# Attention and MLP on one core: heads in pairs on the full array, zero-padded keys, attention merged with the preceding batch's MLP

## The chip, the cores and the metric

The kernel runs on one core of a Trainium2 chip. The metric is device time in microseconds (us), the median of several executions. The engines have short names in the profile: PE (TensorE, matrix products), PEld (its weight loads), DVE (VectorE), ACT (ScalarE), POOL (GpSimd) and SP (SyncE, which here only issues loads and stores). "Span" is the time from a profiled execution's first instruction to its last; the time of an execution is about 2 us more. The numbers of the profile are of one profiled execution of each kernel.

## The reference, cut to what matters

```python
# q, k, v: (8 batches, 12 heads, 448 positions, 64), float32
q_n, k_n = rmsnorm(q, g_q), rmsnorm(k, g_k)          # over the 64, with 1e-6
scores = q_n @ k_n.T / 8;  attn = softmax(scores)
x = (attn @ v) laid out as (3584 tokens, 768)
h = x @ w_in                                         # 768 -> 2048
g = h * clip(h + 3, 0, 6) / 6
out = g @ w_out                                      # 2048 -> 768, float32
```

## The kernel before

It takes a batch at a time. First it loads all twelve heads and finds all their norms, then it runs through the heads one by one, and between the heads it places pieces of the MLP of the batch before. Positions are cut into four tiles of 112. Both weights are loaded first, ahead of q and k, and cast on POOL.

```python
for kt in range(NKT):                                    # both weights, before any q or k
    nc.sync.dma_start(out=st[:], in_=moe_w_in[...])
    nc.gpsimd.tensor_copy(out=w_in_sb[:, kt, :], in_=st[:])
...
for h in range(H):                                       # loads and squares of all heads
    ...
    nc.gpsimd.tensor_tensor(out=sq[:], in0=qk_sb[:], in1=qk_sb[:], op=A_MULT)       # L190
    nc.vector.tensor_reduce(out=ssq_all[:, h, :], in_=sq[:], axis=X, op=A_ADD)      # L191
nc.scalar.activation(out=rstd_all, in_=ssq_all, func=LN, ...)    # then EXP, scale -0.5
...
# per head: transposes of q and k (L225, L227), then for each of 4 key tiles
nc.tensor.matmul(out=sc_ps[:], lhsT=kT[:, j * PP:(j + 1) * PP], rhs=qpT[:], ...)    # L241: 64 rows
nc.scalar.activation(out=eT[:], in_=sc_ps[:], func=EXP, scale=rstd_all[...])        # L246
# 16 products of probabilities and values (L258), then the division (L265, L266)
...
# MLP pieces of batch b-1 between the heads: h (L103), activation (L110, L111), y (L125)
```

## Time and profile before

| | before |
|---|---|
| time, median of 4 runs beside the changed kernel | 773.21 us (768.98 to 775.74) |
| PE busy, 0 to 75 us | 0.8 us |
| PE busy, 200 to 300 us | 99.0 us |
| one batch in the middle | about 77 us |

The first lines are the page's first part (busy time of each engine over the span) and its slices, each of 1/40 of the span, with the busy share in tenths:

```profile
span 768.0 us, 12093 instructions
...
PE 643.1 (84%) x4672; PEld 388.0 (51%) x4672; DVE 356.5 (46%) x946; ACT 358.3 (47%) x608; POOL 136.3 (18%) x222
...
PE   0000999698999999998999899989999999987566
...
POOL 5544311232411211121112111210000000000000
```

PE does nothing for four slices and is then nearly always busy. The windows view gives the same by stage, with the number of instructions behind each busy time, then the granted TensorE clock (1.00 is full speed; this trace has no clock records before 160 us, where the view says 1.00), the DMA share and GB/s:

```profile
0.00:75.00 75.00, 0.80 (x9) 0.80 (x10) 22.58 (x42) 3.22 (x4) 38.26 (x54) 1.00 0.79 232
200.00:300.00 100.00, 99.00 (x782) 61.28 (x781) 61.64 (x164) 58.34 (x100) 21.69 (x35) 1.00 0.32 79
```

The waits view (who waited for whom: total us, times, longest) says what the start is: one single wait, for the scaled queries, that come only after all norms of a batch and after both weights.

```profile
PE qkT_ps L225 <- DVE qs_bf L209: 74.2, 1, 74.2
```

The groups by shape (line, engine, operation, output<-inputs, shapes, count, then busy us and mean ns of one, and idle time before with its releasers) give what the operations take:

```profile
L103 PE MATMUL h_ps<-xT_sb,w_in_sb 128*128 128x448 bf16 x768 | 177.0, 362 | 25.4 <-DVE gT L111 24.8 <-DVE xT_sb L299 0.5
L241 PE MATMUL sc_ps<-qpT,kT 64*112 64x448 bf16 x384 | 141.4, 416 | 10.5 <-DVE kT L233 7.5 <-ACT eT L246 3.1
...
L258 PEld LDWEIGHTS <-eT 112*112 112x112 bf16 x1536 | 101.9, 141 | 51.2 <-issue 21.2 <-PE sc_ps L241 20.3 <-PE qkT_ps L227 2.0
L190 POOL TENSOR_TENSOR sq<-qk_sb 112x512 f32<-112x512 f32 x96 | 101.5, 1062 | 146.2 <-DMA qk_sb<-in_k_dram 95.6 <-DVE qs_bf L209 20.4 <-DVE ssq_all L191 19.3
...
L103 PEld LDWEIGHTS <-w_in_sb 128*128 128x128 bf16 x768 | 69.9, 100 | 93.7 <-issue 45.5 <-POOL v_aug L217 1.0
```

A matmul's recorded time is longer than its share of a stream of matmuls (362 ns for L103 above, with starts 189 ns apart), so I also took the distance from each matmul's start to the start of the next in the trace. Medians from 200 to 600 us: 189 ns within L103 (448 columns), 52 ns within L258, 49 ns within a run of transposes. The score matmul L241 also streams 448 columns, but with 64 rows: its median is 279 ns.

### The profile page before, as it was taken

The numbers are of one execution on the slowest core, as the hardware profiler recorded it, in microseconds if no ns is written. First come the engines' busy times: TensorE is split into PE (matmuls) and PEld (weight loads), VectorE is DVE, ScalarE is ACT, GpSimd is POOL, SyncE is SP. The second block draws the span as 40 slices with busy tenths as digits, with TensorE's granted clock in tenths as the row PEclk, the third lists the DMA queues.
The fourth block names the chain that finished last, engine by engine and source line by source line (L and its number), as shares of the span: only waits on it lengthen the run. The fifth ranks groups of instructions, "written<-read, shape, count | busy, mean of one in ns | idle before, by whom it ended". The sixth has DMA issues, their size and how long they took to land.

```text
span 768.0 us, 12093 instructions
## 1 busy us (share of the span) xinstructions
PE 643.1 (84%) x4672; PEld 388.0 (51%) x4672; DVE 356.5 (46%) x946; ACT 358.3 (47%) x608; POOL 136.3 (18%) x222
## 2 busy tenths in 40 slices
PE   0000999698999999998999899989999999987566
PEld 0000565354566556655665566556755665554234
DVE  1226535767846763666357643754255324411210
ACT  0001446357655673566456644664466546621221
POOL 5544311232411211121112111210000000000000
PEclk9999999999999999999999989998999999999999
DMA  7787701714433323331333223320100010011001
GB/s 277 239 219 188 164 1 33 159 32 104 102 81 84 79 49 93 82 72 45 79 91 73 54 60 92 80 54 25 46 10 1 19 55 2 1 37 36 1 18 54
DMA packets 141113, 57.41 MB, mean 75 GB/s; under 512 B 134656, under 2 KB 134656, under 8 KB 140288
## 3 DMA queue, kind: packets, MB, share of 16 engines
q1 hardware_dynamic: 141056, 56.65, 28.6%
q8 instruction: 36, 0.59, 0.3%
q14 instruction: 21, 0.17, 0.1%
HBM read 45.61 MB, written 11.01 MB: 74 GB/s over the span
## 4 chain that ended last, share of the span: by engine, by line
PE 79%; DMA 6%; ACT 6%; DVE 5%; POOL 2%; issue 1%; SPq 0%; ACTq 0%; DVEq 0%; POOLq 0%
PE y_ps L125 22%; PE h_ps L103 20%; PE sc_ps L241 15%; PE av_ps L258 13%; PE qkT_ps L225 4%; PE qkT_ps L227 3%; DMA wst_out<-in_moe_w_out_dram 3%; DMA wst_in<-in_moe_w_in_dram 2%; DVE gT L111 2%; ACT t_sb L110 2%; PE xT_ps L294 2%; DVE qs_bf L209 1%; ACT L201 1%; ACT L197 1%; ACT y_sb L131 1%
## 5 line engine op out<-in xcount | busy, mean ns | idle before, releaser
L246 ACT ACTIVATE eT<-sc_ps,rstd_all 112x448 bf16<-112x448 f32 x384 | 230.7, 632 | 84.5 <-PE sc_ps L241 82.8
L125 PE MATMUL y_ps<-w_out_sb,gT 128*112 128x256 bf16 (+1 forms) x1024 | 197.3, 329 | 9.6 <-ACT y_sb L131 7.2
L103 PE MATMUL h_ps<-xT_sb,w_in_sb 128*128 128x448 bf16 x768 | 177.0, 362 | 25.4 <-DVE gT L111 24.8
L241 PE MATMUL sc_ps<-qpT,kT 64*112 64x448 bf16 x384 | 141.4, 416 | 10.5 <-DVE kT L233 7.5
L125 PEld LDWEIGHTS <-gT 128*112 128x112 bf16 x1024 | 120.4, 130 | 58.9 <-issue 16.1
L111 DVE SCALAR_TENSOR_TENSOR gT<-t_sb,h_ps 128x448 bf16<-128x448 f32 x128 | 78.9, 617 | 143.2 <-ACT t_sb L110 102.1
L110 ACT ACTIVATE t_sb<-h_ps,half_c 128x448 f32<-128x448 f32 x128 | 81.1, 634 | 122.1 <-PE h_ps L103 113.8
L258 PEld LDWEIGHTS <-eT 112*112 112x112 bf16 x1536 | 101.9, 141 | 51.2 <-issue 21.2
L190 POOL TENSOR_TENSOR sq<-qk_sb 112x512 f32<-112x512 f32 x96 | 101.5, 1062 | 146.2 <-DMA qk_sb<-in_k_dram 95.6
L258 PE MATMUL av_ps<-v_aug,eT 112*112 112x65 bf16 x1536 | 118.8, 228 | 0.3 <-ACT eT L246 0.3
L103 PEld LDWEIGHTS <-w_in_sb 128*128 128x128 bf16 x768 | 69.9, 100 | 93.7 <-issue 45.5
L225 PE MATMUL qkT_ps<-identity,qs_bf 112*64 112x112 bf16 x384 | 44.8, 234 | 74.2 <-DVE qs_bf L209 74.2
L131 ACT COPY y_sb<-y_ps 112x512 f32<-112x512 f32 x64 | 30.6, 479 | 128.7 <-PE y_ps L125 106.5
L191 DVE TENSOR_REDUCE ssq_all<-sq 112x8 f32<-112x512 f32 x96 | 64.2, 675 | 41.5 <-POOL sq L190 41.1
L225 PEld LDWEIGHTS <-qs_bf 112*64 112x64 bf16 x384 | 26.8, 118 | 92.5 <-DVE qs_bf L209 74.2
L241 PEld LDWEIGHTS <-kT 64*112 64x112 bf16 x384 | 41.9, 132 | 60.7 <-issue 39.2
L217 POOL MEMSET v_aug<- 112x4 bf16 x96 | 10.3, 117 | 283.9 <-PE av_ps L258 276.2
L209 DVE TENSOR_TENSOR qs_bf<-qk_sb,rstd_all 112x256 bf16<-112x256 f32 x96 | 42.4, 460 | 26.9 <-ACT rstd_all L201 17.0
L231 DVE TENSOR_SCALAR qpT<-qkT_ps,gprime 64x448 bf16<-64x448 bf16 x96 | 42.0, 438 | 27.4 <-PE qkT_ps L227 21.4
L265 DVE RECIPROCAL rden<-av_ps 112x4 f32<-112x4 f32 x96 | 17.3, 180 | 79.7 <-PE av_ps L258 79.7
L215 DVE CAST k_bf<-qk_sb 112x256 bf16<-112x256 f32 x96 | 36.2, 380 | 34.0 <-DMA qk_sb<-in_k_dram 34.0
L227 PE MATMUL qkT_ps<-identity,k_bf 112*64 112x112 bf16 x384 | 45.6, 232 | 0.0
(24 smaller groups left out, 240.9 us busy)
## 6 DMA issues: line engine op xcount, KB each, us to landing
qk_sb<-in_q_dram SPq DMA_DIRECT2D x96, 112.0 KB, 2.6
qk_sb<-in_k_dram SPq DMA_DIRECT2D x96, 112.0 KB, 2.7
v_sb<-in_v_dram SPq DMA_DIRECT2D x96, 112.0 KB, 2.2
out_dram<-y_sb SPq DMA_DIRECT2D x32, 336.0 KB, 2.7
wst_in<-in_moe_w_in_dram SPq DMA_DIRECT2D x6, 1024.0 KB, 5.1
wst_out<-in_moe_w_out_dram SPq DMA_DIRECT2D x16, 384.0 KB, 3.8
gq_t<-in_g_q_dram SPq DMA_DIRECT2D x1, 0.2 KB, 2.3
gk_t<-in_g_k_dram SPq DMA_DIRECT2D x1, 0.2 KB, 2.3
```

The costliest lines, as they stand in the source:

```text
L103: nc.tensor.matmul(out=h_ps[:], lhsT=w_in_sb[:, kt, f * 128:(f + 1) * 128], rhs=xT_sb[:, kt, bb * S:(bb + 1) * S], start=(kt == 0), stop=( ...
L110: nc.scalar.activation(out=t_sb[:], in_=h_ps[:], func=RELU, bias=half_c[:, :], scale=1.0 / 6.0)
L111: nc.vector.scalar_tensor_tensor(out=gT[:, f, :], in0=t_sb[:], scalar=1.0, in1=h_ps[:], op0=A_MIN, op1=A_MULT,)
L125: nc.tensor.matmul(out=y_ps[:], lhsT=gT[:, f, mt * PP:(mt + 1) * PP], rhs=w_out_sb[:, f, n0:n1], start=(f == 0), stop=(f == NFT - 1),)
L190: nc.gpsimd.tensor_tensor(out=sq[:], in0=qk_sb[:], in1=qk_sb[:], op=A_MULT)
L191: nc.vector.tensor_reduce(out=ssq_all[:, h, :], in_=sq[:], axis=mybir.AxisListType.X, op=A_ADD,)
L209: nc.vector.tensor_tensor(out=qs_bf[:], in0=qk_sb[:, 0:NJ, :], in1=rstd_all[:, h, 0:NJ].unsqueeze(2).to_broadcast([PP, NJ, D]), op=A_MULT,)
L225: nc.tensor.transpose(qkT_ps[:, j * PP:(j + 1) * PP], qs_bf[:, j, :], identity[:])
L227: nc.tensor.transpose(qkT_ps[:, (NJ + j) * PP:(NJ + j + 1) * PP], k_bf[:, j, :], identity[:])
L241: nc.tensor.matmul(out=sc_ps[:], lhsT=kT[:, j * PP:(j + 1) * PP], rhs=qpT[:], start=True, stop=True,)
L246: nc.scalar.activation(out=eT[:], in_=sc_ps[:], func=EXP, bias=0.0, scale=rstd_all[:, h, NJ + j:NJ + j + 1],)
L258: nc.tensor.matmul(out=av_ps[:, i, 0:D + 1], lhsT=expT[j][:, i * PP:(i + 1) * PP], rhs=v_aug[:, j, :], start=(j == 0), stop=(j == NJ - 1),)
```

## The change

Its intent is to fill the array. Two heads form a pair, so that q and k of a pair have 128 rows; the keys of one head of the pair are padded with zeros in the rows of the other, so that each score matmul runs over the full array. Positions are cut into three tiles of 128, and the last 64 positions ("odd rows") of both heads share one tile. The attention's output comes out by token and is normalised with one division per pair. MLP work goes in small pieces between the attention's pieces, in proportion to its cost. The weights are cast by the DMA, the norms are found on POOL with a power instead of on ACT, and the scaling of q and k moves from DVE to POOL. (Nearly the whole body is new; this is its core.)

```diff
-    nc.scalar.activation(out=rstd_all[:], in_=ssq_all[:], func=LN, ...)
-    nc.scalar.activation(out=rstd_all[:], in_=rstd_all[:], func=EXP, bias=0.0, scale=-0.5)
+    def rstd_of(ssq, n):
+        nc.gpsimd.tensor_scalar(ms[:], ssq, 1.0 / D, 1e-6, A_MULT, A_ADD)              # L128
+        nc.gpsimd.tensor_tensor(out=rs[:], in0=ms[:], in1=npow[:, 0:n], op=A_POW)      # L130
+    def load_pair(P): ...                                                              # L138, L141
+    def prep_pair(P):
+        nc.gpsimd.tensor_tensor(out=sq[:], in0=qk_flat, in1=qk_flat, op=A_MULT)        # L150
+        nc.vector.tensor_reduce(out=ssq[:], in_=sq..., axis=AX_X, op=A_ADD)            # L152
+        rs = rstd_of(ssq[:], 4 * NT)
+        for i in range(2):
+            nc.gpsimd.tensor_tensor(out=qks[:, i]..., in0=qk[:, i]..., in1=rs4...)     # L158
+        nc.gpsimd.tensor_copy(out=va[:, :, :, 0:D], in_=vf...)                         # L164
+    def trans_pair(P):                      # 6 transposes (L241), q copied (L243)
+        for a in range(2):                  # keys times 1 or 0 by half: the padding
+            nc.vector.tensor_scalar_mul(kp[:, a, :], ps[:, 1]..., gmask[:, a:a + 1])   # L247
+    def score(P, u):                        # 7 a pair
+        nc.tensor.matmul(out=ps[:], lhsT=lhsT, rhs=st["qT", b][:, j, :], ...)          # L263
+        nc.scalar.activation(out=st["e", P][:, u, :], in_=ps[:], func=EXP, ...)        # L264
+    # av: products with the values (L272, L275), division (L289, L291); xtrans (L329, L330)
-qk_pool bufs=H, bf_pool bufs=H
+qk_pool = pool("qk_pool", 4);  qks_pool = pool("qks_pool", 4);  sq_pool = pool("sq_pool", 2)
+    def att_items(P):
+        items = [(0.0, lambda: load_step(P + 4)), (0.0, lambda: prep_step(P + 3)),
+                 (0.36, lambda: trans_step(P + 2))]
+        ...                                 # score(P + 1, u) merged with av(P, t), xtrans(P)
+    for P in range(4): load_step(P)
+    for kt in range(NKT): nc.gpsimd.dma_start(out=w_in_sb[:, kt, :], in_=moe_w_in[...])  # casts
+    for P in range(3): prep_step(P)
+    for ft in range(0, NFT, 4): nc.gpsimd.dma_start(out=w_out_sb[...], in_=moe_w_out[...])
+    for b in range(B):
+        mlp = merge(h_items(b - 1), y_items(b - 2))
+        for _, fn in merge(att, mlp): fn()
```

## The prediction

> **What bounds the kernel now.** TensorE, after a late start. The chain of waits is 79% PE, and the windows show PE 98 to 99% busy from 200 to 600 us, DVE 47 to 62%, ACT 56 to 58%, POOL 5 to 22%. In the first 75 us PE is busy 0.8 us: weights are loaded ahead of q and k, and the first transpose waits 74.2 us (waits view) for the normalised queries of all twelve heads. Later a batch takes about 77 us. From matmul start to next matmul start the trace has, as medians, 189 ns for L103 (448 columns), 215 and 109 ns for L125 (512, 256), 52 ns for L258, 49 ns for a transpose, but 280 ns for the score matmul L241, which also streams 448 columns with 64 rows: about 90 ns more than a full-height one, x384 = 35 us.
>
> **What changes, in PE time, estimated from those distances.**
> - Scores: 384 x 280 ns = 107 us become 336 x 189 = 64 us: heads of a pair share one full-height tile, and the 64 odd keys of both heads make one matmul.
> - Attention x values: 1536 x 52 = 80 us become 1344 x about 50 = 67 us. The Trainium skill, "TensorE: Matmul & The Clock Gate", section "Weight-path perf modes", says fast weight load needs 128 weight columns. The trace agrees: 100 to 107 ns for 128 columns, 130 to 141 ns for 112.
> - Transposes: 960 x 49 = 47 us become 504 x 56 = 28 us.
> - h: same columns, 145 us. y: 28 row tiles instead of 32, 166 us become 896 x 162 = 145 us.
> Sum 545 before, 449 after: 56 us a batch. I add 8% for idle: about 61 us a batch against 77.
>
> **What moves.** DVE's scaling and casts go to POOL, weight casts into the DMA; the Ln/Exp table loads (19 us of ACT) go. The weights are loaded behind the first pairs, so attention starts near 25 us. But POOL then has per pair: square 1.55 us (1062 ns for 512 elements), power (not in this trace; I guess 1 us), two scalings of 0.85 us, a value cast of 0.5 us, and a wait for DVE's reduction of 1 us: about 6.5 us. The skill's "GPSIMD Engine Reference", section 4.1, calls two-input work about 2x slower than on VectorE; no run here compares it. PE without MLP needs 3.5 us a pair, so batch 0 runs at POOL's (and the loads') pace, and batch 1, which has only h to fill it, is near balance. From batch 2 PE (10 us a pair) binds.
>
> **Time.** Batch 0 ends near 75 us, batch 1 near 120; six batches of 61 us: 486; h of the last batch with y of the last two, 57 us: 543; end 3 us, and 6 us between span and time: about **550 us**. Range 505 to 600. Chances: faster 0.985, same 0.01, slower 0.005.
>
> **What would show it.** Score matmuls near 190 ns apart; first score near 25 to 30 us; in the windows, POOL over 80% busy and PE under 60% up to 75 us, and PE above 95% from 130 us; batches 58 to 64 us long; ACT near 320 us and DVE near 270 us busy.
>
> **What would make it wrong.** A power of several microseconds makes POOL the bound throughout (600 us or more). Weight transfers could starve the pair loads in batch 0. The single transpose buffer could stall PE 1 us twice a pair (12 us a batch). A faster POOL shrinks batches 0 and 1: 510 us.

## The result, and the profile after

| | before | after |
|---|---|---|
| time, median of 4 runs each | 773.21 us | 674.27 us (673.27 to 674.56) |
| ratio, fast runs of the same rounds | 1 | 0.8735 (95%: 0.8694 to 0.8777) |
| PE busy | 643.1 us | 493.8 us |
| POOL busy | 136.3 us | 357.7 us |
| mean granted clock | 0.991 | 0.913 |

Ratios here are the mean time of one kernel's fast runs over that of the other's of the same rounds, so they are not quite the ratio of the medians. The change is 12.6% faster, but 674 us lies far above the 550 us predicted and outside the range.

The page's first part and slices (the clock in tenths), after:

```profile
span 672.3 us, 9839 instructions
...
PE 493.8 (73%) x3848; PEld 290.1 (43%) x3848; DVE 245.9 (37%) x544; ACT 295.9 (44%) x521; POOL 357.7 (53%) x362
...
PE   0026354742869767978788868797879999999997
...
POOL 2499699999796766546355684646455210000000
PEclk9999675877889978998789779999999999999999
```

The stages, after:

```profile
75.00:130.00 55.00, 26.94 (x217) 16.75 (x218) 17.64 (x39) 20.69 (x37) 52.02 (x49) 0.69 0.32 90
130.00:200.00 70.00, 39.74 (x342) 25.09 (x342) 31.28 (x71) 27.60 (x50) 63.68 (x59) 0.81 0.30 80
...
300.00:400.00 100.00, 77.26 (x577) 44.32 (x577) 40.82 (x88) 43.91 (x78) 59.09 (x56) 0.87 0.20 58
...
500.00:600.00 100.00, 97.83 (x822) 58.69 (x820) 41.73 (x97) 65.19 (x115) 19.51 (x24) 1.00 0.12 39
```

PE is busy 25% of the first 75 us, 49 and 57% of the next two stages, about four fifths of the time from 200 to 500 us, and full only from 500 us on. The groups that answer to those of before:

```profile
L130 POOL TENSOR_TENSOR rs<-ms,npow 128x12 f32<-128x12 f32 x56 | 127.3, 2274 | 3.2
L263 PE MATMUL s_ps<-qT,kp 128*128 128x448 bf16 x288 | 101.8, 384 | 9.5 <-DVE kp L247 4.3 <-DVE qT L226 4.1 <-ACT eT L264 0.7
L158 POOL TENSOR_TENSOR qks<-qk,rs 128x384 bf16<-128x384 f32 x96 | 77.5, 828 | 25.5 <-PE t_ps L241 24.6
...
L150 POOL TENSOR_TENSOR sq<-qk 128x768 f32<-128x768 f32 x48 | 70.4, 1466 | 108.3 <-DMA qk<-in_k_dram 107.8
L272 PEld LDWEIGHTS <-eT 128*128 128x128 bf16 x1152 | 69.1, 103 | 36.1 <-issue 8.5 <-ACT eT L264 1.0 <-DVE xn L291 0.7
L152 DVE TENSOR_REDUCE ssq<-sq 128x12 f32<-128x768 f32 x48 | 45.7, 951 | 170.8 <-POOL sq L150 170.8
```

The matmuls themselves did what was predicted or better: the median distance from 300 to 590 us is 189 ns for a score matmul (279 before), 33 ns for a product with the values (52 before) and 56 ns for a transpose of 128 columns. What was not predicted: the power L130 takes 2.27 us, and DVE's reduction L152 is preceded by 171 us of idle time. The waits:

```profile
DVE ssq L152 <- POOL sq L150: 170.8, 44, 11.2
...
POOL sq L150 <- DMA qk<-in_k_dram: 107.8, 28, 15.2
...
PE xt_ps L329 <- DVE xn L291: 41.2, 14, 7.0
...
POOL qks L158 <- PE t_ps L241: 24.6, 15, 3.5
```

To put the time on a map, I took from the trace the end of each batch (start of the last division of its six pairs, L291) and set it against the prediction:

| | predicted | measured | difference |
|---|---|---|---|
| batch 0 done | 75 us | 122 us | +47 |
| batch 1 takes | 45 us | 66 us | +21 |
| batches 2 to 7 take | 366 us (61 each) | 415 us (78, 73, 81, 67, 61, 55) | +49 |
| rest of the span | 60 us (57 and an end of 3) | 69 us | +9 |

The differences sum to 126 us; the 2 us between span and time, where I had counted 6, and the rounding of 552 to 550 bring that to the 124 us of the miss. The last two batches, in which only three pairs are left to prepare (the last square starts at 510 us), run at the predicted pace or better. So what fails has to do with the preparation of later pairs. This is a stretch of the timeline (start us, duration us, engine, line, idle before and its releaser), first DVE, then POOL:

```profile
274.43 0.55 DVE L356 SCALAR_TENSOR_TENSOR gT_2479<-t_sb,h_ps 128x384 bf16<-128x384 f32 x1 [0.99 <-ACT t_sb L354]
276.86 0.20 DVE L289 RECIPROCAL rd<-x_ps 128x6 f32<-128x6 f32 x1 [1.88 <-PE x_ps L275]
278.71 0.95 DVE L152 TENSOR_REDUCE ssq<-sq 128x12 f32<-128x768 f32 x1 [1.65 <-POOL sq L150]
279.58 0.55 DVE L291 TENSOR_TENSOR xn<-x_ps,rd 128x384 bf16<-128x384 f32 x1
```

```profile
272.48 1.62 POOL L158 TENSOR_TENSOR qks<-qk,rs 128x384 bf16<-128x384 f32 x2 [1.64 <-PE t_ps L241]
277.21 1.47 POOL L150 TENSOR_TENSOR sq<-qk 128x768 f32<-128x768 f32 x1 [3.11 <-DMA qk<-in_k_dram]
279.75 0.20 POOL L128 TENSOR_SCALAR ms<-ssq 128x12 f32<-128x12 f32 x1 [1.08 <-DVE ssq L152]
```

The division of a pair consists of a reciprocal (L289) and a product (L291). The reciprocal runs at 276.86 us, and 0.2 us later the product could follow. But next in DVE's order stands a reduction of squares (L152) of a much later pair. POOL has only begun that square at 277.21 us, because it waited 3.11 us for the load. So the product comes at 279.58 us, 2.5 us late, and with it the transpose of the attention's output on PE and all that stands behind it there, the transposes of the next pair's q and k included. These free the buffer of scaled pairs that POOL's L158 waits for (1.64 us), L158 frees the buffer of loaded pairs that the next load waits for, and so on to the next square. It is a closed loop through DVE, PE, POOL and the load queue. (PE had other work and idled only 0.76 us here for the product; over the run such waits are the 41.2 us of the waits above.) By counting DVE's records I find that the reduction of pair n runs ahead of the product of pair n-10 in the middle of the run, while the program's text has it ahead of pair n-3 (preparation of pair P+3 in the step of pair P). Four buffers of loaded and four of scaled pairs let the scheduler run that far. The stretch shown is one case of several. Of the 48 reductions 11 stand between a reciprocal and its product (30.5 of the 170.8 us of waiting), 10 directly ahead of a reciprocal (43.4 us), 11 ahead of the MLP's product gT (33.5 us) and 9 ahead of a copy of q (31.4 us). PE's idle time that DVE ended is 108 us in the whole run: 44 us for gT, 41 us for the division, 14 us for the copies of the transposed output and 8 us for others.

### The profile page after: what moved, and what is told of

Its sections match the earlier page's. It is cut to its first block, busy times and chain, and to the rows that moved or that the text cites. A ratio compares the mean times of both kernels' runs of the same rounds, so it can differ in the third digit from the quotient of the medians.

```text
span 672.3 us, 9839 instructions
## 1 busy us (share of the span) xinstructions
PE 493.8 (73%) x3848; PEld 290.1 (43%) x3848; DVE 245.9 (37%) x544; ACT 295.9 (44%) x521; POOL 357.7 (53%) x362
## 4 chain that ended last, share of the span: by engine, by line
POOL 35%; PE 30%; DMA 13%; DVE 8%; SPq 5%; issue 4%; ACT 3%; POOLq 0%; ACTq 0%
PE h_ps L349 13%; DMA qk<-in_k_dram 12%; PE y_ps L366 11%; POOL rs L130 11%; POOL sq L150 10%; POOL qks L158 8%; DVE ssq L152 4%; SPq L174 3%; PE s_ps L263 2%; ACT t_sb L354 2%; PE t_ps L241 2%; SPq L138 1%; POOL qkrs L205 1%; POOL ms L128 1%; DMA vr<-in_v_dram 1%
## 5 line engine op out<-in xcount | busy, mean ns | idle before, releaser
L264 ACT ACTIVATE eT<-s_ps,zero_c 128x448 bf16<-128x448 f32 x336 | 200.7, 634 | 117.9 <-PE s_ps L263 113.6
L354 ACT ACTIVATE t_sb<-h_ps,half_c 128x384 f32<-128x384 f32 (+1 forms) x128 | 81.0, 634 | 140.6 <-PE h_ps L349 136.2
L130 POOL TENSOR_TENSOR rs<-ms,npow 128x12 f32<-128x12 f32 x56 | 127.3, 2274 | 3.2
L150 POOL TENSOR_TENSOR sq<-qk 128x768 f32<-128x768 f32 x48 | 70.4, 1466 | 108.3 <-DMA qk<-in_k_dram 107.8
L263 PE MATMUL s_ps<-qT,kp 128*128 128x448 bf16 x288 | 101.8, 384 | 9.5 <-DVE kp L247 4.3
L152 DVE TENSOR_REDUCE ssq<-sq 128x12 f32<-128x768 f32 x48 | 45.7, 951 | 170.8 <-POOL sq L150 170.8
L158 POOL TENSOR_TENSOR qks<-qk,rs 128x384 bf16<-128x384 f32 x96 | 77.5, 828 | 25.5 <-PE t_ps L241 24.6
L272 PEld LDWEIGHTS <-eT 128*128 128x128 bf16 x1152 | 69.1, 103 | 36.1 <-issue 8.5
L329 PE MATMUL xt_ps<-identity,xn 128*128 128x128 bf16 x144 | 19.1, 245 | 41.2 <-DVE xn L291 41.2
L349 PE MATMUL h_ps<-xT_990,w_in_sb 128*128 128x512 bf16 x96 | 29.3, 423 | 12.2 <-DVE gT_1655 L356 11.7
L349 PE MATMUL h_ps<-xT_2600,w_in_sb 128*128 128x512 bf16 x96 | 29.2, 420 | 6.9 <-DVE gT_3402 L356 6.4
L349 PE MATMUL h_ps<-xT_422,w_in_sb 128*128 128x384 bf16 x96 | 26.6, 376 | 7.1 <-DVE gT_905 L356 7.1
L349 PE MATMUL h_ps<-xT_1771,w_in_sb 128*128 128x384 bf16 x96 | 24.1, 363 | 9.8 <-DVE gT_2479 L356 9.6
```

Of the source, the lines that this page charges most:

```text
L130: nc.gpsimd.tensor_tensor(out=rs[:], in0=ms[:], in1=npow[:, 0:n], op=A_POW)
L150: nc.gpsimd.tensor_tensor(out=sq[:], in0=qk_flat, in1=qk_flat, op=A_MULT)
L152: nc.vector.tensor_reduce(out=ssq[:], in_=sq[:].rearrange("p (n d) -> p n d", d=D), axis=AX_X, op=A_ADD)
L158: nc.gpsimd.tensor_tensor(out=qks[:, i].rearrange("p t h d -> p h t d"), in0=qk[:, i].rearrange("p h (t d) -> p h t d", d=D), in1=rs4[:, i ...
L263: nc.tensor.matmul(out=ps[:], lhsT=lhsT, rhs=st["qT", b][:, j, :], start=True, stop=True)
L264: nc.scalar.activation(out=st["e", P][:, u, :], in_=ps[:], func=EXP, bias=zero_c[:], scale=1.0)
```

## The experiments

Theories: (A) POOL's throughput is the bound, above all the power; (B) the fixed order on DVE closes the loop described; (C) the low granted clock is a cause of its own; (D) the early weight loads delay the start. Each call of four or two kernels had its own runs of the kernel before. The calls ran on four different chips, and the mean of the fast runs of before was 769 to 772 us in them (773 us beside the changed kernel). So a difference in us between kernels of different calls, or to the changed kernel, is good to some 4 us only; the ratios allow for it.

| run | what | time, us | ratio to before |
|---|---|---|---|
| (the change) | | 674.27 | 0.8735 |
| e1_cheap_pow | multiplication for power (wrong) | 610.86 | 0.7957 |
| e2_reduce_in_order | reductions keep their place | 583.37 | 0.7588 |
| e3_weights_later | first weight after three pairs | 667.21 | 0.8682 |
| e4_all_three | e1 + e2 + e3 (wrong) | 530.79 | 0.6904 |
| e5_more_buffers | 6 buffers for 4 | 664.54 | 0.8622 |
| e6_cheap_power_in_order | e1 + e2 (wrong) | 540.69 | 0.7010 |
| e7_in_order_weights_power24 | e2 + e3, odd rows' powers joined | 567.52 | 0.7355 |
| e8_less_on_pool | e7, and three POOL tasks on DVE | 559.08 | 0.7248 |
| e9_rsqrt_on_dve | e7, reciprocal root on DVE | 579.60 | 0.7523 |
| e10_rsqrt_and_less_on_pool | e8 and e9 | 581.19 | 0.7543 |
| e11_one_pair_earlier | e8, prepared one pair earlier | 542.57 | 0.7032 |
| e12_earlier_values_on_pool | e7, prepared one pair earlier | 550.53 | 0.7134 |

### e1_cheap_pow: the power's size alone

```diff
-        nc.gpsimd.tensor_tensor(out=rs[:], in0=ms[:], in1=npow[:, 0:n], op=A_POW)
+        nc.gpsimd.tensor_tensor(out=rs[:], in0=ms[:], in1=npow[:, 0:n], op=A_MULT)
```

> The power on POOL becomes a multiplication (a wrong result on purpose); the order of all instructions on all engines is the same as in the changed kernel. Theory A (POOL's throughput, with a power of 2.27 us per pair, is what went wrong): POOL loses about 2.1 us x 56 = 118 us; the power has 11% of the chain that ended last, 74 us, so about 600 us. Theory B (from 200 to 520 us not POOL's throughput but a loop through buffers and DVE's fixed order holds the pace; only the first 200 us are POOL's): some 20 powers come off the path, about 630 us, and the pairs between 250 and 450 us still take above 11 us.

The order of the instructions is the same on all five engines, so only the duration differs. The groups by shape, with the power a multiplication:

```profile
L152 DVE TENSOR_REDUCE ssq<-sq 128x12 f32<-128x768 f32 x48 | 45.7, 951 | 124.6 <-POOL sq L150 124.5
...
L130 POOL TENSOR_TENSOR rs<-ms,npow 128x12 f32<-128x12 f32 x56 | 12.0, 214 | 3.2
```

The power is worth 2274 - 214 = 2060 ns, or 2.06 us, a piece, 115 us of POOL's time, and 63 us of the kernel's (674.27 to 610.86). Batches 0 and 1 end at 150 instead of 188 us; the batches after that still take 67, 69, 70, 66, 61 and 55 us, and DVE's reduction still waits 125 us. The time lies between the two expectations and nearer to A's (600 and 630 us). So A is a part of the truth: it sets the pace at the start. For the later batches it isn't enough, as B says: their pairs still take 11 to 12 us in batches 2 to 5.

### e2_reduce_in_order: the place of the reductions

```diff
-        nc.vector.tensor_reduce(out=ssq[:], in_=sq..., axis=AX_X, op=A_ADD)
+        tc.keep_in_program_order(nc.vector.tensor_reduce(out=ssq[:], in_=sq..., axis=AX_X, op=A_ADD))
```

(The same for the odd rows' reduction. The call pins an instruction behind what the text writes before it on its engine; it adds no work.)

> Only DVE's order is changed: each reduction of squares stays behind what the program writes before it, instead of being moved ahead of the softmax division of an earlier pair. Theory A (POOL's throughput): within 1%, 668 to 680 us. Theory B (DVE waits in order for a square whose load has hardly landed, and PE's transposes wait behind DVE): the pairs between 200 and 520 us take 9.7 us instead of 11.4, 28 pairs, about 48 us less: 625 us; DVE's wait of the reduction for the square falls from 171 us to under 60 us, and the granted clock in 200 to 500 us rises above 0.96. Theory C (the low granted clock is a cause of its own) expects the clock to stay near 0.9.

It gained 91 us, nearly twice what B expected. The reduction of pair n now runs ahead of the division of pair n-3, as in the text. Its group and a window:

```profile
L152 DVE TENSOR_REDUCE ssq<-sq 128x12 f32<-128x768 f32 x48 | 45.4, 945 | 20.7 <-POOL sq L150 20.4
```

```profile
300.00:400.00 100.00, 94.18 (x783) 57.22 (x781) 49.73 (x109) 59.76 (x106) 71.17 (x68) 0.95 0.27 80
400.00:500.00 100.00, 99.11 (x839) 59.70 (x836) 50.44 (x111) 65.47 (x115) 52.92 (x55) 1.00 0.20 60
```

DVE's idle time before the reduction fell from 171 to 21 us, while POOL's power is as slow as before. PE's idle time that DVE ended fell from 108 to 11 us, that which POOL ended rose from 60 to 85 us; in all PE idles 73 us less, and its busy time, for the same matmuls, is 18 us shorter. Batches 2 to 7 take 56, 64, 57, 65, 57 and 54 us instead of 78, 73, 81, 67, 61 and 55, and batches 0 and 1 end at 158 instead of 188 us. The clock in the window from 400 to 500 us is 1.00 (0.98 in the changed kernel), from 300 to 400 us 0.95 (0.87) and from 200 to 300 us 0.97 (0.91), though nothing was done for it. That speaks against C: the clock was low because PE stood idle. The Trainium skill, "TensorE: Matmul & The Clock Gate", section "Part 1: The HAM clock gate", says that the array's clock is gated by how busy it was recently. The trace of the changed kernel agrees: with PE busy 27 of 55 us (75 to 130 us) the clock was 0.69. That a low clock also lengthened the loop a little is not excluded; no run separates it. The pin also changed the planned order on the other engines, as the scheduler lays its plan anew. On POOL this matters. In the changed kernel, from pair 23 on, all but two squares stand directly behind the scaling that frees their own load's buffer, so POOL waits out each load: 93 us in all before the squares after the first. With the pin eight or more POOL instructions stand between, and 9 us of that wait are left. So this run alone doesn't prove that DVE's place is what counts. e5 below speaks to it, as there POOL's wait for loads nearly goes away by itself; but no run pins DVE and keeps POOL's order.

### e3_weights_later: the start

```diff
-    for kt in range(NKT):
-        nc.gpsimd.dma_start(out=w_in_sb[:, kt, :], in_=moe_w_in[kt * 128:(kt + 1) * 128, :])
     for P in range(3):
         prep_step(P)
+    for kt in range(NKT):
+        tc.keep_in_program_order(nc.gpsimd.dma_start(out=w_in_sb[:, kt, :], in_=moe_w_in[...]))
```

> The loads of the first weight are issued after POOL's work on the first three pairs. Theory D (the loads of the first pairs share the transfer engines with 6 MB of weights, so the first square starts at 20.6 us instead of about 8): first square near 8 us, total about 12 us less, 662 us, as POOL sets the pace from there on. Rival: the blocked queue of the load instructions (13 us in one issue of the 256-byte rows of the odd keys) is the cause: first square still at 18 us or later, total unchanged. Third possibility: the weights then come too late for the first h and the gain is given back.

The first square starts at 11.7 instead of 20.6 us, and the kernel is 7 us faster by the medians, 4 us by the ratios, where 12 us were expected. (That is 1% or less, and the two intervals of the ratios overlap, so the times alone don't settle it; between e6 and e4 below, where they don't overlap, the same edit is worth 10 us by the medians and 8 us by the ratios.) (The scheduler moved one load of the second weight to the front in exchange, so the transfers of the start were not quite free of weights.) The rival fell: it expected the first square at 18 us or later. The load queue's long stand at the odd rows' loads is an effect of the same crowding. The load queue's own lines, the changed kernel first, then this run:

```profile
6.60 16.31 SPq L174 DMA_DIRECT2D qkr<-in_k_dram  x2
```

```profile
7.15 5.12 SPq L174 DMA_DIRECT2D qkr<-in_k_dram  x2
```

### e4_all_three and e6_cheap_power_in_order: what is left

The edits are those of e1, e2 and e3 together, and those of e1 and e2.

> Cheap power (wrong result on purpose), reductions in program order and weights later together. If the three causes are the whole of the miss, the time is near the 550 us that were predicted, 540 to 570 us, with PE above 95% busy from 130 us. If something else also holds PE back it is above 580 us.

> Cheap power (wrong result on purpose) and reductions in program order, weights as in the changed kernel. If power and order cost independently: 672 - 63 - 90 = 519 us. If both cost partly the same time (each frees the same wait): 535 to 550 us, and the difference to the kernel with all three is the price of the early weights, 7 us as measured alone.

With all three the kernel takes 531 us, 19 us less than predicted; with cheap power and order alone it takes 541 us. Batches 2 to 7 take 55, 57, 57, 57, 57 and 54 us in both, and the windows of e4 show PE full from 200 us on:

```profile
200.00:300.00 100.00, 97.94 (x836) 59.05 (x835) 54.11 (x118) 64.89 (x113) 53.60 (x76) 1.00 0.33 92
300.00:400.00 100.00, 98.06 (x842) 59.78 (x841) 53.86 (x118) 65.59 (x115) 47.16 (x71) 1.00 0.31 91
```

So power, order and early weights are the whole of the miss, and more: together they cost 143 us (674 to 531), where the miss is 124 us. Power and order are not additive: 63 and 91 us alone, but 134 us together. Each of them shortens the same waits.

### e5_more_buffers: is it the order, or a lack of buffers?

```diff
-    qk_pool = pool("qk_pool", 4)
+    qk_pool = pool("qk_pool", 6)
-    qks_pool = pool("qks_pool", 4)
+    qks_pool = pool("qks_pool", 6)
```

> Buffers of the loaded and of the scaled pairs 4 to 6 each, nothing else by hand. Theory B (the reduction stands too early in DVE's fixed order; its place is as far ahead as the buffers let the planned order run) expects no gain: the reduction of a pair moves still further ahead of the division that follows it, middle batches stay at 70 us or above, 665 to 690 us, and DVE's wait of the reduction for the square stays above 140 us. The rival (simply too few buffers between PE's transposes and the loads) expects middle batches of 57 to 65 us and about 600 us.

Ten us were gained (664.54 us), where the rival expected 74. Batches 2 to 7 take 73, 69, 76, 63, 58 and 55 us. By the same count as before, the reduction of pair n now runs ahead of the product of pair n-14, and DVE still waits for it:

```profile
DVE ssq L152 <- POOL sq L150: 162.0, 45, 11.3
```

More buffers moved the reduction further ahead, and the wait stayed. PE's idle time that DVE ended is 108 us, as in the changed kernel, though POOL's wait for loads before the squares fell from 93 to about 25 us without the first square (it waits longer for PE instead). The lack of buffers falls as the main cause, POOL's wait for loads can't be the whole of it either, and B stands with e2. Not all that B expected came: 63 and 58 us in two late batches show that the longer lead did help there.

### e7_in_order_weights_power24 and e8_less_on_pool: how far POOL still counts

e7 has the edits of e2 and e3, with the two powers of the odd rows joined:

```diff
-            rs = rstd_of(ssq[:], H)                 # in the loop over q and k: 12 columns each
+        rs = rstd_of(ssq[:], 2 * H)                 # once, 24 columns
```

> Correct kernel: reductions in order, weights later, and the two powers of the odd rows (12 columns each) made one of 24 columns. If the power costs per column it takes 4.5 us, if it is mostly fixed about 2.5 us. Time: 583 of the reductions in order, less 7 for the weights and 0 to 10 for the powers: 568 to 577 us.

The power costs by the column. (4172 - 2277) / 12 = 158 ns a column, so 0.38 us is fixed, and joining them saves nearly nothing (the kernel takes 567.5 us, the low end of what was expected):

```profile
L130 POOL TENSOR_TENSOR rs<-ms,npow 128x12 f32<-128x12 f32 x48 | 109.3, 2277 | 0.2
...
L130 POOL TENSOR_TENSOR rs<-ms,npow 128x24 f32<-128x24 f32 x4 | 16.7, 4172 | 0.0
...
L201 POOL TENSOR_TENSOR sqr<-qkr 128x768 f32<-128x768 f32 x8 | 11.7, 1468 | 1.5 <-DMA qkr<-in_q_dram 1.0
```

e8 moves three tasks to DVE, each kept in its place there:

```diff
-            nc.gpsimd.tensor_tensor(out=sq[:], in0=src, in1=src, op=A_MULT)       # odd rows' squares
+            tc.keep_in_program_order(nc.vector.tensor_tensor(out=sq[:], in0=src, in1=src, op=A_MULT))
-        nc.gpsimd.tensor_copy(out=va[:, :, :, 0:D], in_=vf...)                    # values
+        tc.keep_in_program_order(nc.vector.tensor_copy(out=va[:, :, :, 0:D], in_=vf...))
-            nc.gpsimd.tensor_scalar(vbd[...], vr[:], mask[:, a:a + 1], None, A_MULT)
+            tc.keep_in_program_order(nc.vector.tensor_scalar(vbd[...], vr[:], mask[:, a:a + 1], None, A_MULT))
```

> As the one before, and DVE instead of POOL casts the values, masks the odd rows' values and squares the odd rows (about 0.5 us a pair and 5 us every two batches off POOL, whose busy time falls from 358 to about 300 us). If POOL's throughput is what is left of the miss in batches 0 and 1 and in every second batch (64 us against 57): about 545 us with all later batches at 57 to 58 us. If DVE's added waits for loads give it back: 570 us or more.

It gave 8 us, not 22. POOL's busy time fell to 306 us as planned, batch 1 ends at 138 instead of 145 us, but every second batch still takes 61.5 us and the others 58.5. So POOL's sum of work is not what is left there: the every-second-batch pattern stays with 50 us less of it. The same square of 768 columns takes 1468 ns on POOL (e7, above) and 951 ns on DVE:

```profile
L202 DVE TENSOR_TENSOR sqr<-qkr 128x768 f32<-128x768 f32 x8 | 7.6, 951 | 0.5 <-DMA qkr<-in_k_dram 0.4 <-DMA qkr<-in_q_dram 0.2
```

The Trainium skill, "GPSIMD Engine Reference", section "4.1 Engine selection", gives about 2x for two-input work.

### e9_rsqrt_on_dve and e10_rsqrt_and_less_on_pool: a way without the power

```diff
+        pin(nc.vector.tensor_scalar(hb[:], ms[:].bitcast(I32), 1, None, arith_shift_right))   # L132
+        pin(nc.vector.tensor_scalar(y[:].bitcast(I32), hb[:], -1.0, float(0x5f3759df), A_MULT, A_ADD))
+        for it in range(2):                          # Newton: y = y * (1.5 - 0.5 * ms * y * y)
+            ...                                      # three instructions each
```

> Correct kernel without the power: the reciprocal root is found on DVE by shifting the bits and two Newton steps, nine instructions on 12 columns of an estimated 0.15 to 0.2 us (a reciprocal of 6 columns took 0.19 us), 1.4 to 1.8 us a pair; reductions in order, weights later. POOL loses 2.5 us a pair and the wait for DVE and back. If POOL's power is the whole rest of the miss and DVE has room (half of a batch idle): middle batches 57 to 58 us and 530 to 545 us. If the added DVE time delays the copies PE waits for: middle batches above 60 us, 555 us or more.

> The same, and DVE also casts the values and handles the odd rows' squares and masks, as in the run with less on POOL. DVE then has about 6 us of work more a batch on top of some 38. If POOL still limits batches 0 and 1: 5 to 10 us less than the run before. If DVE is now the tighter of the two: the same or slower.

Both results are correct, and both miss: 579.6 and 581.2 us, 12 us more than with the power on POOL (e7). DVE, with nine more instructions on PE's way, became the place where it waits: PE's idle time that DVE ended is 48 us in e9 and 57 us in e10, against 8 us in e7. In e9 the middle batches take 62 to 66 us, though the clock is at 0.98 to 1.00 there. One reason was not in the estimate. Some of these instructions on 12 columns take 0.16 us and some up to 1.46 us. The timeline of e9, POOL and DVE:

```profile
177.77 0.17 DVE L130 TENSOR_SCALAR ms<-ssq 128x12 f32<-128x12 f32 x1
177.82 1.47 POOL L165 TENSOR_TENSOR sq<-qk 128x768 f32<-128x768 f32 x1 [1.82 <-DVE ssq L167]
...
177.98 1.33 DVE L132 TENSOR_SCALAR hb<-ms 128x12 int32<-128x12 int32 x1
...
179.35 0.17 DVE L135 TENSOR_SCALAR rs<-hb 128x12 int32<-128x12 int32 x1
```

The shift (L132) starts 0.16 us after POOL's square and ends at 179.31 us, with the square's end at 179.29. The Trainium skill, "SBUF — State Buffer", section "Who interferes with whom", says that DVE in its two-port modes and POOL share ports under an exclusive lock, and that the loser is fully blocked. Of the 48 shifts of 12 columns in this trace, the 17 that took over 0.2 us each overlapped an instruction of POOL that reads SBUF and ended 0.03 to 0.04 us after it; of the other 31, at 0.16 to 0.17 us, all but one overlapped none. That the lock is the reason is taken from the page; these runs show the coincidence.

### e11_one_pair_earlier and e12_earlier_values_on_pool: lead instead of throughput

```diff
-    qk_pool 4, qks_pool 4, v_pool 3, NVA = 4
+    qk_pool 5, qks_pool 5, v_pool 4, NVA = 5
-        items = [(0.0, lambda: load_step(P + 4)), (0.0, lambda: prep_step(P + 3)), ...
+        items = [(0.0, lambda: load_step(P + 5)), (0.0, lambda: prep_step(P + 4)), ...
```

(and five loads and four preparations ahead of the loop; everything else as in e8 and e7)

> As the run with less on POOL (559 us), but every pair is prepared one pair earlier (with one buffer more for the loaded, scaled and value tiles). If the 61.5 us of every second batch come from POOL's work arriving unevenly (odd rows of two batches at once) and not from its sum (63% busy), a longer lead evens it out: all later batches 57 to 59 us, about 545 us. If the waits between DVE and POOL set the pace, nothing changes: 555 to 562 us.

> The same longer lead on the correct kernel that keeps values, masks and squares on POOL (567.5 us, every second batch 63 to 64 us, POOL 72% busy there). Same question: 550 to 555 us if the unevenness is the cause, 565 to 570 us if not. It should be slower than the other one in batches 0 and 1, where POOL is the limit.

Both gained 17 us, and every later batch now takes 55 to 59 us. That fits unevenness as what was left in every second batch: the odd rows of two batches arrive at once, and a lead of three pairs did not carry POOL over them. (A longer lead would also hide slow hand-overs between DVE and POOL; that only every second batch was slow speaks for the odd rows. No run moves the odd rows alone.) In batches 0 and 1, where POOL's sum counts, e11 is ahead as expected: batch 1 ends at 124 us, in e12 at 141 us. e11 is correct, takes 542.57 us, and is the fastest correct version: 0.7032 of the kernel before (95%: 0.6998 to 0.7066) over five rounds. Its page (31 of its 3848 matmuls have no record in this trace):

```profile
PE 461.6 (85%) x3817; PEld 277.9 (51%) x3848; DVE 289.8 (54%) x616; ACT 296.5 (55%) x521; POOL 307.2 (57%) x283
...
PE   0107768789999998999999998999999999999996
...
PEclk9999798989999999999999999999999999999999
```

## Why the prediction was wrong

- **The kind of gain was right.** "Faster" was given 0.985, and both matmul costs and pace came true where nothing held PE back. Scores: 189 ns apart, as predicted. Values: 33 ns where "about 50" stood, so that term is 1152 x 33 + 192 x 56 ns = 49 us instead of 67. What the skill's page says of weights of 128 columns agrees with the loads themselves, 103 ns against 141 ns for 112 columns; but the rows of these matmuls grew from 112 to 128 as well, and no run separates the two. With the three causes removed (e4) a batch took 57 us, where 61 stood. So the estimate was 19 us too high in its other terms, which hid a part of the 143 us that the causes cost; that the miss looked no larger was luck.
- **First failing step: "power (not in this trace; I guess 1 us)".** It measured 2.27 us. This term of POOL's sum was mis-sized, and with it "about 6.5 us" a pair. The sum also named no work for the odd rows (squares, powers, scalings and masks), which took POOL 63 us in the changed kernel, 1.3 us a pair. e1 prices the power at 63 us of the kernel's time as it stood; part of that is not POOL's throughput but its share in the loop. The risk was on the list ("POOL the bound throughout"), but in the stages from 200 us on POOL was 62% busy at most.
- **Second failing step: "From batch 2 PE (10 us a pair) binds."** This was concluded from adding up each engine's work as if each could run when it has work. Between 200 and 500 us no engine was full: PE was busy 77 to 85% and POOL 53 to 62%. The wait was made by the fixed order, which placed reductions up to ten pairs ahead on DVE, in front of divisions, copies and MLP products that PE waited for (108 us), and squares on POOL directly behind the scaling that frees their load's buffer. e2, which changes the order and no work, gained 91 us; e5 shows that buffers are not the cure. The "wait for DVE's reduction of 1 us" was counted on POOL only; what counted was DVE's wait for POOL, 171 us.
- **Third failing step: "attention starts near 25 us".** The first score matmul began at 48 us. The first load of k was issued at 3.9 us but the first square started at 20.6 us, as the loads of the weights and of the odd rows were all on their way at once (e3 shows it for the weights; the odd rows' part was not tested). The list of risks named the starving of pair loads, but the estimate had no room for it. e3 prices the early first weight at 7 us by the medians and 4 us by the ratios; in e4, with cheap power, the first score began at 29.6 us.
- **The rest of the span** was 69 us instead of 60: in the changed kernel 100 h and 228 y matmuls stood behind the last division (100 x 215 + 228 x 162 ns = 58 us), which took 64 us, and 5 us followed the last matmul's start. It is 69 us in e4 too, so it belongs to PE's work and not to the causes above.
- **A risk that did not come true:** PE's wait for the single transpose buffer was seen (14 us in five waits for the copy of the transposed output), but not at 12 us a batch.
- **Views that were right or wrong:** ACT at 296 and DVE at 246 us were near the 320 and 270 predicted. "PE above 95% from 130 us" was wrong for the changed kernel, and right for e4 (97.9 and 98.1 us of 100 in its windows). Up to 75 us PE was under 60% (25%), but POOL at 65% and not over 80%; batches took 55 to 81 us and not 58 to 64.

What stays open: how much of the gain of e2 comes from DVE's new order and how much from that on POOL and PE, which the scheduler made along with it, and how much a low clock lengthened the loop.

## What to carry to other kernels

Adding up each engine's work gives the pace only if the fixed order on every engine fits the real arrival of its inputs. Where a lightly loaded engine shows a large wait in front of one instruction, see what stands behind that instruction in its order: here keeping a reduction in its written place, which drew POOL's squares back too, was worth 91 us, more than taking a third of POOL's busy time away (e1), and more buffers were no substitute. An operation with no duration in the trace (here the power) is best measured alone before a sum is built on it.

## What the Trainium skill lacked or had wrong

- "GPSIMD Engine Reference" has no cost for a power: here 2.27 us for 12 columns and 4.17 us for 24, about 158 ns a column, against 0.21 us for a multiplication of the same 12 columns.
- The same page, section "4.1 Engine selection", has two-input work about 2x slower than on VectorE; a square of 768 float32 columns (one tile as both inputs) was 1.54 times slower (1468 against 951 ns).
- "TensorE: Matmul & The Clock Gate", section "Why this matters for your kernels", gives a single matmul of 32 rows the same time as one of 128. Neither this page nor "TensorEngine Tiling (Array Packing)" gives in ns what a change of shape between neighbours costs. In the kernel before, a full-height h matmul (L103) was followed after 189 ns by its like but after 282 ns by a 64-row score matmul, and such a score matmul was followed after 233 ns by its like and after 326 ns by an h matmul (medians from 200 to 600 us).
- No page shows what cost most here: an instruction moved ahead in an engine's fixed order, whose input comes late, holds up unrelated work behind it (171 us of DVE's waits, 108 us of PE's idle time that DVE ended).
